# A recurrent scan beside a gated block: opening moments moved to ScalarE, B loaded ahead of the second weight part, fewer warming products

## The chip, the cores and the metric

The kernel runs on one core of one Trainium2 chip. The metric is the device time of one execution in microseconds (us), as the median of several executions. The engines are TensorE (PE; its weight loads are a row of their own, PEld), VectorE (DVE), ScalarE (ACT), GpSimd (POOL) and SyncE (SP), whose queue issues nearly all DMAs here.

## The reference, cut to what matters

The input x has 2048 tokens of 448 features. It is normalised, and the result goes through two branches whose outputs are multiplied and added to x:

```python
def reference(...):
    xn = _layernorm(x, axis=-1)              # (x - mean) / sqrt(var + 1e-5)
    # branch A: complex diagonal recurrence over the tokens, 448 states
    Lam_bar = exp(dt * Lam)
    Bu = xn @ (((Lam_bar - 1) / Lam)[:, None] * Bmat).T
    h[t] = Lam_bar * h[t-1] + Bu[t]
    s = 2 * (h @ Cmat.T).real + xn * Dskip
    # branch B: gated block, 448 -> 1792 -> 448
    z = (sigmoid(xn @ w_gate) * (xn @ w_up)) @ w_down
    return x + s * silu(z)
```

All inputs and the output are bf16.

## The kernel before, in words

The 2048 tokens are cut into four chunks of 512, and each chunk into four tiles of 128 tokens. For a chunk the work is: moments and normalisation of its four tiles, a turn of the normalised tiles into `xnT` (features on the partitions), the gate and up products (14 feature tiles `ft`, a gate bank `g_ps` and an up bank `u_ps` each, `gu_mm` and `emit_gu`), the products with B (`emit_bu`, four state tiles `pt`), the rotations and scans on VectorE, and one chunk later the down products (`emit_down`), the products with C (`emit_y`) and the output.

Every engine runs its instructions in the order in which the Python code emits them; `keep_order` at the end pins that order. Nothing is reordered at run time, so an instruction that waits holds up all that stands behind it on its engine. The same holds for the SP queue, which issues the loads, the transposes by DMA and the stores. Small pieces of work for later chunks are put beside the gate and up products by a planner with fixed costs (`at`, `later`, `fill`); it is not touched here.

The change concerns the opening, that is the first chunk up to its gate and up products.

- **Loads.** SP issues, in this order: x tiles 1 and 2 (one DMA, `x_t[0][:, 0:2]`), x tiles 3 and 4 (one DMA), then `load_w(sync, 0, 512)`: columns 0 to 512 of the gate and up weights (four DMAs, for feature tiles `ft` 0 to 3), `load_w(sync, 512, 1024)` (four DMAs, for `ft` 4 to 7), x of chunk 1 (`load_x(1)`), and B in two halves `b_re` and `b_im` (two DMAs each). ACT issues four small loads of parameter rows. Later SP issues the transposes of B into `bT` (`emit_b`, one for each `pt` and half), with the third weight part, columns 1024 to 1792 (`load_w(sync, 1024, F)`), between those of `pt` 0 and those of `pt` 1.
- **Warming products.** `warm(n)` lets TensorE multiply the identity n times into a bank that nobody reads. There are three groups: 33, 36 and 14 products.
- **Moments.** `ln_stats(t)` takes mean and variance of a tile on VectorE (`bn_stats`, then `bn_aggr`). `ln_root` adds epsilon on VectorE (tile `ve`) and takes the root on GpSimd (`sd`); `ln_scale` takes the reciprocal on VectorE; `ln_norm` normalises on VectorE; `ln_turn` turns a tile on TensorE into the bank `tp_x` (five transposes) and `ln_out` copies it to `xnT`. Tiles 1 and 2 go first, tiles 3 and 4 later.
- **Constants of the scan.** `emit_vecs` turns the parameter rows on TensorE (`tp_v`), copies them on VectorE and takes an exponential on ACT (`dt_b`); `emit_angles` forms `theta`, `turn` and `arg_r` on VectorE. `emit_whole` rounds an angle on ACT, `emit_frac` takes the fraction on VectorE, `emit_sin` and `emit_cos` take sine and cosine on ACT.

TensorE's order in the opening is: 33 warming products, the turn of the rows, 36 warming products, the turns of tiles 1 and 2, 14 warming products, then the products of `ft` 0 and 1 for the first 256 tokens (tiles 1 and 2), the turns of tiles 3 and 4, `ft` 2 and 3 for the first 256 tokens, `ft` 0 to 3 for the other 256, and then whole feature tiles with the products of B between them: `ft` 4, 5, B for `pt` 0, `ft` 6, 7, B for `pt` 1, `ft` 8, 9, B for `pt` 2 and so on.

Of the kernel before, what the change touches and what calls it, by code (L numbers as in the profile page):

```python
# [10 lines left out]
FP32 = mybir.dt.float32  # L11
BF16 = mybir.dt.bfloat16
I32 = mybir.dt.int32
ALU = mybir.AluOpType
ACT = mybir.ActivationFunctionType

S_TOK = 2048
D = 448
F = 1792
P = 128  # L20
TC = 512
HC = TC // 2
NCH = S_TOK // TC
TPC = TC // P
KT = 4
# [5 lines left out]
EPS = 1e-5  # L31
# [32 lines left out]
def kernel(  # L64
# [18 lines left out]
    pe, act, dve, pool, sync = nc.tensor, nc.scalar, nc.vector, nc.gpsimd, nc.sync  # L83
    w = ctx.enter_context(tc.tile_pool(name="w", bufs=1))
# [3 lines left out]
    fp = ctx.enter_context(tc.tile_pool(name="fp", bufs=4))  # L88
# [7 lines left out]
    x_t = [w.tile([P, TPC, D], BF16, name=f"x{c}", tag=f"x{c}") for c in range(3)]  # L96
# [18 lines left out]
    def load_rows(eng, t, mat, f0, f1):  # L115
        eng.dma_start(out=t[:, 0:3, f0:f1], in_=mat[0:384, f0:f1].rearrange("(kt p) f -> p kt f", p=P))
        eng.dma_start(out=t[0:64, 3, f0:f1], in_=mat[384:448, f0:f1])

    def load_w(eng, f0, f1):
        for t, mat, p0 in ((wg, B_w_gate, 0), (wu, B_w_up, 64)):  # L120
            eng.dma_start(out=t[:, :, f0:f1], in_=mat[0:384, f0:f1].rearrange("(kt p) f -> p kt f", p=P))  # L121
            eng.dma_start(out=wt[p0:p0 + 64, f0:f1], in_=mat[384:448, f0:f1])  # L122
# [13 lines left out]
    load_row(act, 3, A_Dskip)  # L136
    sync.dma_start(out=x_t[0][:, 2:4, :], in_=x_src[:, 2:4, :])
    load_w(sync, 0, 512)
    load_w(sync, 512, 1024)
    raw = {}  # L140

    def load_x(c):
        if c == 3:
            x_t.append(w.tile([P, TPC, D], BF16, name="x3", tag="tc_re"))
        sync.dma_start(out=x_t[c][:], in_=x_src[:, c * TPC:(c + 1) * TPC, :])

    load_x(1)
    for nm, mat in (("b_re", A_B_re), ("b_im", A_B_im)):
        raw[nm] = w.tile([P, KT, DP], BF16, name=nm, tag="raw" + nm[1:])
        dve.memset(raw[nm][:, :, D:DP], 0.0)  # L150
        load_rows(sync, raw[nm], mat, 0, D)

    ctr = {}

# [34 lines left out]
    def warm(n):  # L189
        for _ in range(n):  # L190
            pe.matmul(warm_ps[:], lhsT=ident[:], rhs=ident[:], start=True, stop=True)  # L191

    def turn_twice(o, src, n):

        for kt in range(3):
            pe.transpose(o[:, kt, :], src[:, kt * P:(kt + 1) * P], ident[0:n, 0:n])
        pe.transpose(o[:, 3, :], src[:, D - P:D], ident[0:n, 0:n])
        pe.transpose(o[0:64, 3, :], src[:, 384:D], ident[0:n, 0:n])


    mv = w.tile([P, NT, 2], FP32, name="mv")
# [3 lines left out]
    def ln_stats(t):  # L205
        stats = cp.tile([P, 6], FP32, name="stats")
        dve.bn_stats(out=stats[:], in_=x_t[t // TPC][:, t % TPC, :])  # L207
        dve.bn_aggr(out=mv[:, t, :], in_=stats[:])

    def ln_root(c, j0=0, n=TPC, sd=None):  # L210
        t0 = c * TPC + j0
        ve = cp.tile([P, TPC, 1], BF16, name="ve")
        dve.tensor_single_scalar(out=ve[:, 0:n, :], in_=mv[:, t0:t0 + n, 1:2], scalar=EPS, op=ALU.add)
        if sd is None:
            sd = cp.tile([P, TPC, 1], BF16, name="sd")
        pool.tensor_tensor(out=sd[:, j0:j0 + n, :], in0=ve[:, 0:n, :], in1=half[:, 0:n, :], op=ALU.pow)
        return sd
# [33 lines left out]
    def ln_out(j, tp, copy):  # L251
        copy(out=xnT[0][:, :, j * P:(j + 1) * P], in_=tp[:])  # L252


    def emit_b(cc, pt):
        n = P if pt < 3 else 64
        if cc == 0:
            p0 = pt * P
        else:
            p0 = D if pt == 3 else 512 + pt * P  # L260
        sync.dma_start_transpose(out=bT[:, :, p0:p0 + n], in_=raw[("b_re", "b_im")[cc]][0:n, pt, :])
# [13 lines left out]
    def emit_vecs():  # L275
        tp = ps.tile([P, KT, 4], BF16, name="tp_v", tag="g")
        turn_twice(tp, rows, 4)
        vec = w.tile([P, KT, 4], FP32, name="vec")
        dve.tensor_copy(out=vec[:], in_=tp[:])
        dt_b = w.tile([P, KT], BF16, name="dt_b")  # L280
        act.activation(dt_b[:], vec[:, :, 0], ACT.Exp)
        K.update(dt=dt_b, lim=vec[:, :, 1], lre=vec[:, :, 2], dsk=vec[:, :, 3])

    def emit_angles():
        theta, arg_r, turn, r_col = col("theta"), col("arg_r"), col("turn"), col("r_col")
        dve.tensor_tensor(out=theta[:], in0=K["dt"][:], in1=K["lim"], op=ALU.mult)
        dve.tensor_single_scalar(out=turn[:], in_=theta[:], scalar=1.0 / TWO_PI, op=ALU.mult)
        dve.tensor_tensor(out=arg_r[:], in0=K["dt"][:], in1=K["lre"], op=ALU.mult)
        K.update(arg=arg_r)
        K.update(theta=theta, turn=turn, r=r_col)  # L290
# [69 lines left out]
    def emit_whole(pt, eng):  # L360
        whole = sp.tile([P, HC], I32, name="whole", tag=("ta", "tb")[pt % 2])
        if eng is act:
            act.activation(whole[:], iota_f[:], ACT.Copy, scale=K["turn"][:, pt:pt + 1])
        else:
            dve.tensor_scalar(out=whole[:], in0=iota_f[:], scalar1=K["turn"][:, pt:pt + 1], scalar2=None,
                              op0=ALU.mult)
        K[pt] = whole
# [228 lines left out]
    def gu_out(c, ft, gt, ub, ut=None):  # L596
        sig = fp.tile([P, TC], BF16, name="sig")
        act.activation(sig[:], gt[:], ACT.Sigmoid)  # L598
        if ut is up_copy:
            up_copy(ft)  # L600
        elif ut is not None:
            act.copy(out=ub[:], in_=ut[:])  # L602
        emit_mul()

        def mul():
            h = fp.tile([P, TC], BF16, name="hF", bufs=23)
            dve.tensor_tensor(out=h[:], in0=sig[:], in1=ub[:], op=ALU.mult)  # L607
            hF[c, ft] = h

        due.append(mul)  # L610
# [77 lines left out]
    def ln_plan(c):  # L688
        sd, own = [], c - 1
        for j in range(TPC):  # L690
            at(own, 1 + j, 0.8, lambda j=j: ln_stats(c * TPC + j))
            at(own, 7 + j, 0.0, lambda j=j: ln_norm(c, j))
        at(own, 10, 0.0, lambda: ln_twice(c, act.copy))
        at(own, 5, 0.17, lambda: sd.append(ln_root(c)))
        at(own, 6, 0.35, lambda: ln_scale(c, sd[0]))

    dummy = w.tile([P, 1], FP32, name="dummy")
    act.activation(dummy[:], hpi[:], ACT.Exp)
    warm(33)
    ln_stats(0)  # L700
    ln_stats(1)
    emit_vecs()
    warm(36)
    sd0 = ln_root(0, 0, 2)
    ln_stats(2)
    emit_angles()
    tps = {}

    def norm0(j):
        ln_norm(0, j)  # L710
        tps[j] = ln_turn(0, j)
# [1 line left out]
    ln_scale(0, sd0, 0, 2)  # L713
    norm0(0)
    norm0(1)
    warm(14)
    emit_whole(0, act)
    emit_whole(1, act)
    ln_out(0, tps[0], act.copy)
    emit_whole(2, act)  # L720
    emit_whole(3, act)
    act.activation(K["r"][:], K["arg"][:], ACT.Exp)
    ln_stats(3)
    ln_root(0, 2, 2, sd0)
    ln_out(1, tps[1], dve.tensor_copy)
    emit_frac(0)
    emit_sin(0)
# [36 lines left out]
    ln_stats(TPC + 1)  # L764
    gu_out(0, 2, gus[2][0], ubs[2], up_copy)
    gu_out(0, 3, gus[3][0], ubs[3], up_copy)
    for cc in range(2):
        emit_b(cc, 0)
    load_w(sync, 1024, F)
    for pt in range(1, KT):  # L770
        for cc in range(2):
            emit_b(cc, pt)
    sd1 = []

    for j in range(2, TPC):
# [51 lines left out]
    c = NCH - 1  # L827
# [38 lines left out]
```

## Time and profile before

| | |
|---|---|
| median of 3 runs | 199.35 us (198.4 to 199.5) |
| profiled execution, device time | 199.56 us |
| its span, first to last instruction | 197.5 us |
| granted TensorE clock, mean | 1.000 |
| busy: PE, DVE, ACT, POOL | 189.9, 158.3, 109.0, 40.5 us |
| DMA moved | 14.86 MB, mean 75 GB/s |

The profile is one execution. Its times run from the first instruction, and some 2.06 us of the device time (199.56 less 197.5) lie outside the span. A line of the timeline gives the start, the duration, the engine, the line of the kernel and the operation with its tiles; several equal instructions in a row are drawn together with "xN". The chain of waits is followed back from the last instruction: each piece is what the end of the program depended on at that time.

### The profile page before, as it was taken

How to read it: one execution, taken by the hardware profiler on the slowest of the kernel's cores; microseconds unless marked ns; L12 is line 12 of the kernel's file. 1: busy time of each engine (PE TensorE's matmuls, PEld its weight loads, DVE VectorE, ACT ScalarE, POOL GpSimd, SP SyncE). 2: the span in 40 equal slices, each digit the busy share in tenths (PEclk: the TensorE clock that was granted, in tenths of full speed). 3: DMA queues.
4: the chain of work that ended last, by engine and by line, in shares of the span. 5: the costliest groups of instructions: out<-in, count | busy, mean ns of one | idle time of the engine just before them, and what ended most of it. 6: DMA issues, size and time to landing. Idle time of an engine off the chain costs nothing.

```text
span 197.5 us, 3152 instructions
## 1 busy us (share of the span) xinstructions
PE 189.9 (96%) x1093; PEld 92.1 (47%) x1108; DVE 158.3 (80%) x325; ACT 109.0 (55%) x206; POOL 40.5 (21%) x93
## 2 busy tenths in 40 slices
PE   7999979999999999999999999999999999999991
PEld 6965424334444444444444444444444444545561
DVE  4899799784989789999974999999619999994223
ACT  3599646674488886344664766346646644341130
POOL 3337498730302201010232031003200000000000
PEclk9999999999999999999999999999999999999999
DMA  5984984899310310521001001330100010020100
GB/s 156 311 256 98 262 110 95 245 294 184 79 32 0 84 36 27 106 71 27 3 0 28 2 0 27 81 98 23 27 3 0 0 27 2 27 72 24 46 23 23
DMA packets 27591, 14.86 MB, mean 75 GB/s; under 512 B 16308, under 2 KB 27576, under 8 KB 27576
## 3 DMA queue, kind: packets, MB, share of 16 engines
q1 hardware_dynamic: 27568, 14.67, 30.7%
q8 instruction: 8, 0.13, 0.3%
q14 instruction: 7, 0.06, 0.1%
q10 hardware_dynamic: 8, 0.00, 0.0%
HBM read 8.38 MB, written 1.84 MB: 52 GB/s over the span
## 4 chain that ended last, share of the span: by engine, by line
PE 88%; DMA 4%; DVE 3%; SPq 1%; issue 1%; ACT 0%; POOL 0%; ACTq 0%; DVEq 0%; POOLq 0%
PE d_ps L623 21%; PE g_ps L585 17%; PE u_ps L585 16%; PE bu L442 11%; PE y_ps L645 9%; PE g_ps L579 7%; PE warm_ps L191 4%; DMA bT<-b_re 4%; PE y_ps L651 1%; PE y_ps L647 1%; DVE ub L757 1%; SPq L121 1%; SPq L122 0%; DVE xnT L252 0%; PE tp_x L243 0%
## 5 line engine op out<-in xcount | busy, mean ns | idle before, releaser
L598 ACT ACTIVATE sig<-g_ps 128x512 bf16<-128x512 f32 x56 | 33.2, 599 | 35.0 <-PE u_ps L579 35.0
L585 PE MATMUL g_ps<-xnT,wg 128*128 128x512 bf16 (+1 forms) x169 | 45.5, 366 | 0.8 <-issue 0.3
L585 PE MATMUL u_ps<-xnT,wu 128*128 128x512 bf16 (+1 forms) x176 | 45.4, 364 | 0.2
L623 PE MATMUL d_ps<-wd,hF 128*128 128x448 bf16 x224 | 45.0, 352 | 0.0
L602 ACT CAST ub<-u_ps 128x512 bf16<-128x512 f32 x52 | 30.3, 583 | 2.1 <-PE u_ps L585 0.4
L623 PEld LDWEIGHTS <-hF 128*128 128x128 bf16 x224 | 21.6, 98 | 20.4
L442 PE MATMUL bu<-xnT,bT 128*128 128x512 bf16 x112 | 26.8, 379 | 1.2 <-DMA bT<-b_re 1.2
L626 ACT ACTIVATE sigd<-d_ps 128x448 bf16<-128x448 f32 x16 | 8.7, 544 | 33.9 <-PE d_ps L623 33.9
L607 DVE TENSOR_TENSOR hF<-sig,ub 128x512 bf16<-128x512 bf16 x56 | 23.6, 423 | 4.0 <-ACT ub L602 3.6
L585 PEld LDWEIGHTS <-wu 128*128 128x128 bf16 x180 | 17.6, 98 | 18.7
L585 PEld LDWEIGHTS <-wg 128*128 128x128 bf16 x180 | 14.5, 97 | 21.6 <-issue 11.9
L472 DVE TENSOR_TENSOR_SCAN wv<-r_col,st,ta 128x512 bf16<-128x512 f32 x18 | 22.5, 1272 | 0.3
L632 DVE TENSOR_TENSOR g_t<-zb,sigd 128x448 bf16<-128x448 bf16 x16 | 6.2, 390 | 19.1 <-ACT zb L628 19.1
L645 PE MATMUL y_ps<-ct,h 128*128 128x448 bf16 (+1 forms) x102 | 21.0, 341 | 0.0
L442 PEld LDWEIGHTS <-bT 128*128 128x128 bf16 x112 | 10.9, 98 | 14.7 <-DMA bT<-b_re 1.7
L579 PE MATMUL g_ps<-xnT,wt 64*128 64x512 bf16 (+1 forms) x60 | 17.2, 367 | 0.0
L579 PE MATMUL u_ps<-xnT,wt 64*128 64x512 bf16 (+1 forms) x60 | 17.2, 367 | 0.0
L453 ACT CAST bus<-bu 128x512 bf16<-128x512 f32 x24 | 13.7, 586 | 6.0 <-PE bu L442 6.0
L479 POOL TENSOR_TENSOR tq<-wv,smT 128x2 f32<-128x2 bf16 x9 | 3.4, 383 | 62.1 <-DVE wv L472 62.1
L207 DVE BATCH_NORM_STATS2 stats<-x 128x6 f32<-128x448 bf16 x16 | 9.9, 617 | 5.0 <-DMA x<-in_A_x_dram 5.0
L645 PEld LDWEIGHTS <-h 128*128 128x128 bf16 x102 | 9.7, 98 | 8.3
L658 DVE TENSOR_TENSOR sg<-y_ps,g_t 128x448 bf16<-128x448 f32 (+1 forms) x17 | 10.0, 587 | 0.7 <-PE y_ps L651 0.2
(125 smaller groups left out, 212.9 us busy)
## 6 DMA issues: line engine op xcount, KB each, us to landing
out_dram<-o_t SPq DMA_DIRECT2D x15, 112.0 KB, 1.7
wd<-in_B_w_down_dram SPq DMA_DIRECT2D x1, 1568.0 KB, 7.9
x<-in_A_x_dram SPq DMA_DIRECT2D x3, 448.0 KB, 3.5
wg<-in_B_w_gate_dram SPq DMA_DIRECT2D x2, 384.0 KB, 5.2
wu<-in_B_w_up_dram SPq DMA_DIRECT2D x2, 384.0 KB
wg<-in_B_w_gate_dram SPq DMA_DIRECT2D x1, 576.0 KB, 4.5
wu<-in_B_w_up_dram SPq DMA_DIRECT2D x1, 576.0 KB, 6.5
bsw<-bus SPq DMA_DIRECT2D x8, 64.0 KB, 2.1
```

The source lines that it names most:

```text
L207: dve.bn_stats(out=stats[:], in_=x_t[t // TPC][:, t % TPC, :])
L442: pe.matmul(pst[:], lhsT=bT[:, kt, lo:hi], rhs=xnT[c][:, kt, :], start=(kt == 0), stop=(kt == KT - 1))
L453: act.copy(out=bus[:, cc, :], in_=pst[:])
L472: dve.tensor_tensor_scan(out=T["wv"][:, cc, :], data0=rb, data1=T["ta"][:, cc, :], initial=(0.0 if c == 0 else st[pt][:, cc, :]), op0=mul, ...
L579: pe.matmul(t[:, n0:n1], lhsT=wt[p0:p0 + 64, f0:f1], rhs=xnT[c][p0:p0 + 64, KT if c == 0 and p0 else 3, n0:n1], start=first, stop=not first)
L585: pe.matmul(t[:, n0:n1], lhsT=wm[:, kt, f0:f1], rhs=xnT[c][:, kt, n0:n1], start=(not first and kt == 0), stop=(first and kt == 2))
L598: act.activation(sig[:], gt[:], ACT.Sigmoid)
L602: act.copy(out=ub[:], in_=ut[:])
L607: dve.tensor_tensor(out=h[:], in0=sig[:], in1=ub[:], op=ALU.mult)
L623: pe.matmul(d[:], lhsT=hF[c, ft][:, j * P:(j + 1) * P], rhs=wd[:, ft, :], start=(ft == 0), stop=(ft == FT - 1))
L645: pe.matmul(y[:, d0:d1], lhsT=hs[c, pt][:, cc, sl], rhs=ct[:, 2 * pt + cc, d0:d1], start=(pt == 0 and cc == 0), stop=False)
L658: dve.tensor_tensor(out=sg[:, d0:d1], in0=ys[c, j][:, d0:d1], in1=gs[c, j][:, d0:d1], op=ALU.mult)
```

## The change

The moments of tiles 3 and 4 are taken by ACT in three steps instead of by VectorE: a copy with a running sum (`ln_sum`), a scaling of both sums to means (`ln_mean`), and the square of the deviation with a running sum (`ln_square`). The root of tiles 1 and 2 is emitted ahead of the parameter vectors. Both copies of the first two turned tiles are on VectorE (one was on ACT before), behind the epsilon step of tiles 3 and 4, and the four `emit_whole` follow each other on ACT. The warming groups are 26, 22 and 11 products. B is loaded ahead of the second weight part and of x of chunk 1, and the third weight part is issued behind the transposes of B for `pt` 1 instead of `pt` 0.

```diff
     load_w(sync, 0, 512)
-    load_w(sync, 512, 1024)
...
-    load_x(1)
     for nm, mat in (("b_re", A_B_re), ("b_im", A_B_im)):
...
         load_rows(sync, raw[nm], mat, 0, D)
+    load_w(sync, 512, 1024)
+    load_x(1)
...
+    sums = w.tile([P, 2, 2], FP32, name="sums")
+
+    def ln_sum(j):
+        junk = fp.tile([P, TC], BF16, name="junk", tag="sig")
+        act.activation(junk[:, 0:D], x_t[0][:, j, :], ACT.Copy, accum_out=sums[:, j - 2, 0:1])
+
+    def ln_mean():
+        act.activation(mv[:, 2:4, 0:1], sums[:, :, 0:1], ACT.Copy, scale=1.0 / D)
+
+    def ln_square(j):
+        junk = fp.tile([P, TC], BF16, name="junk", tag="sig")
+        act.activation(junk[:, 0:D], x_t[0][:, j, :], ACT.Square, bias=mv[:, j, 0:1], scale=-1.0,
+                       accum_out=sums[:, j - 2, 1:2])
+
-    def ln_root(c, j0=0, n=TPC, sd=None):
+    def ln_root(c, j0=0, n=TPC, sd=None, summed=False):
...
-        dve.tensor_single_scalar(out=ve[:, 0:n, :], in_=mv[:, t0:t0 + n, 1:2], scalar=EPS, op=ALU.add)
+        if summed:
+            dve.tensor_scalar(out=ve[:, 0:n, :], in0=sums[:, :, 1:2], scalar1=1.0 / D, scalar2=EPS,
+                              op0=ALU.mult, op1=ALU.add)
+        else:
+            dve.tensor_single_scalar(out=ve[:, 0:n, :], in_=mv[:, t0:t0 + n, 1:2], scalar=EPS, op=ALU.add)
...
-    warm(33)
+    ln_sum(2)
+    ln_sum(3)
+    warm(26)
     ln_stats(0)
     ln_stats(1)
+    sd0 = ln_root(0, 0, 2)
     emit_vecs()
-    warm(36)
-    sd0 = ln_root(0, 0, 2)
-    ln_stats(2)
+    ln_mean()
+    warm(22)
+    ln_square(2)
+    ln_square(3)
     emit_angles()
...
     norm0(0)
     norm0(1)
-    warm(14)
-    emit_whole(0, act)
-    emit_whole(1, act)
-    ln_out(0, tps[0], act.copy)
-    emit_whole(2, act)
-    emit_whole(3, act)
+    warm(11)
+    for pt in range(KT):
+        emit_whole(pt, act)
     act.activation(K["r"][:], K["arg"][:], ACT.Exp)
-    ln_stats(3)
-    ln_root(0, 2, 2, sd0)
+    ln_root(0, 2, 2, sd0, True)
+    ln_out(0, tps[0], dve.tensor_copy)
     ln_out(1, tps[1], dve.tensor_copy)
...
-    for cc in range(2):
-        emit_b(cc, 0)
-    load_w(sync, 1024, F)
-    for pt in range(1, KT):
+    for pt in range(KT):
         for cc in range(2):
             emit_b(cc, pt)
+        if pt == 1:
+            load_w(sync, 1024, F)
```

## The prediction, made before the changed kernel ran

> **What bounds the kernel now.** I read the page's busy times first, then the chain of waits, then the timeline of the opening and the windows.
>
> ```profile
> PE 189.9 (96%) x1093; PEld 92.1 (47%) x1108; DVE 158.3 (80%) x325; ACT 109.0 (55%) x206; POOL 40.5 (21%) x93
> ```
>
> TensorE is idle for 7.6 of 197.5 us. In the chain, and in PE's waits from 26 to 190 us, one hole stands out; the rest is the start, the end and short issue gaps:
>
> ```profile
> PE bu L442 <- DMA bT<-b_re: 1.2, 1, 1.2
> ```
> ```profile
> 8.20 0.56 PE tp_x L243 x10
> 8.76 0.78 PE warm_ps L191 x14
> 9.54 0.38 PE g_ps L585 x3
> ...
> 17.17 0.58 SPq L121
> 17.81 0.48 SPq L122
> 18.33 0.59 SPq L121
> 18.96 0.49 SPq L122
> 19.50 6.99 DMA bT<-b_re
> 26.54 1.90 PE bu L442 x8
> ```
>
> So time can come from two places. Real products begin at 9.44 us (timeline), and all before that on PE is warming or turning. And B for `pt` 1 waits until 26.5 us for a transpose that SP issued at 19.50, behind the third weight part (17.17 to 19.45), and that took 6.99 us to land. Between the two PE has no other wait, so both should add up.
>
> The timeline shows what the start hangs on:
>
> ```profile
> 5.51 0.16 DVE L213 TENSOR_SCALAR ve<-mv 128x2 bf16<-128x2 f32 x1
> 5.58 0.62 DVE L207 BATCH_NORM_STATS2 stats<-x 128x6 f32<-128x448 bf16 x1
> 5.63 0.21 ACT L281 ACTIVATE dt_b<-vec 128x4 bf16<-128x4 f32 x1 [2.03 <-DVE vec L279]
> 5.76 0.73 POOL L216 TENSOR_TENSOR sd<-ve,half 128x2 bf16<-128x2 bf16 x1 [3.44 <-DVE ve L213]
> 6.85 0.70 DVE L230 TENSOR_SCALAR xn<-x,mv,rsd 128x448 bf16<-128x448 bf16 x2
> 8.04 0.72 PE L243 MATMUL tp_x<-ident,xn 128*128 128x128 bf16 x10
> 8.80 0.49 DVE L252 COPY xnT<-tp_x 128x640 bf16<-128x640 bf16 x1 [0.29 <-PE tp_x L243]
> ```
>
> The tiles are normalised by 7.55, but PE turns them at 8.04, because its second warming group ends then. The second copy ends at 9.29 and PE starts 0.15 later.
>
> **The change, part by part.**
>
> *Warming.* The 33 weight loads of the first group take 3.44 us, 0.104 each; the 14 of the third take 0.82, 0.059 each. The 36 of the second take 2.72, which is 13 at the slow pace and 23 at the fast one: the pace rises near 6.7 us. The granted clock is 1.00 in all rows, so only durations show this (mean 313 ns for the first 33, 219 ns for the last 14). With 26 the first group ends at 1.35 + 2.71 = 4.06, and the turn of the rows follows 0.19 later as before, at 4.25. When the rows land isn't shown: not after 4.98, when they are read. Their last issue ends at 2.07 and the shortest landings in the page are 1.5 to 1.7 us, so not before 3.6. I take no wait, since that bound is the nearer small transfer; at 4.98 the turn would come where it is now. The second group runs from 4.59, 22 at 0.105, to 6.90; the turns start at 6.95.
>
> *Root first.* The second `bn_aggr` ends at 5.02. `ve` stood 0.49 behind it, now it follows at 5.06; GpSimd starts 0.25 later, at 5.31, and ends at 6.04. VectorE meanwhile copies `vec` (to 5.31), waits for `dt_b` and makes three angle steps, to about 6.05. Reciprocal 6.08 to 6.24, normalisation from 6.27: xn 1 at 6.62, xn 2 at 6.97. So PE, at 6.95, finds the first tile ready and the second as it gets there.
>
> *Moments on ACT.* VectorE loses two `bn_stats` and two `bn_aggr`, 2 x (0.62 + 0.18) = 1.6 us, and gains one copy of 0.45. ACT gains four passes over 448 elements and one tiny step (0.20, as `dt_b`), and loses the copy of 0.69. The passes aren't in the trace. Nearest rows: 0.53 (`zb`, 448 elements, no pointer), 0.68 (`c_tmp`, one pointer), 0.77 (`xn` on ACT, two pointers); a running sum that is read out separately may add a tiny step of 0.20, so 0.53 to 0.97. No gain below 0.53 is possible, since all three rows have at least this many elements or more operands. I take 0.68, one pointer being what the square has. x of tiles 3 and 4 is issued at 1.23 and lands 2.7 us later, at 3.95; ACT is idle from 3.60 to 5.63. Sums 4.0 to 5.36, `dt_b` to 5.57, means to 5.77, squares to 7.13. Here the change adds a wait: the `ve` of tiles 3 and 4 stands on VectorE ahead of both copies to `xnT`, and PE waits for these. By 0.68 `ve` ends at 7.34, and the first copy can't start before 6.95 + 0.48 = 7.43 anyway (0.48 from first turn to first copy, as now), so the wait is hidden. From 0.71 a pass on it isn't, and each further 0.1 costs 0.4.
>
> [...]
>
> *Copies and start.* Two copies on VectorE take 0.89 (timeline, those of tiles 3 and 4): 7.43 to 8.32. PE starts 0.15 later, at 8.47, against 9.44: **0.97 us gained**. The 11 products end at 8.1. The weights of `ft` 0 to 3 keep their places in the queue: gate is there by 6.95 (SP waited for it) and up by 8.65 (SP issued on its semaphore without a wait), 0.15 before the first up product. Bounds of this term: 0.5 if the rows land as late as 4.98; 0.3 if the turns and the third group run slow (21 at 0.104 from 6.95 end at 9.13); nothing with 0.97 a pass, when squares end at 8.3 and PE starts at 9.55. Behind it ACT keeps step: angles 7.1 to 8.9, table load from 9.1 (10.12 now), the first sigmoid at 15.4 (16.32 now), for a bank PE wants at 16.0 (16.97 now).
>
> *Loads.* SP waits for one landing in eight DMAs back, so its pace (last load issued 9.82 to 10.3) hardly moves; only the order does.
>
> ```profile
> 10.30:14.50 4.20, 4.20 (x46) 2.97 (x42) 3.87 (x14) 4.12 (x9) 0.99 (x4) 1.00 0.85 266
> 14.50:17.20 2.70, 2.70 (x27) 1.91 (x25) 2.64 (x8) 2.67 (x6) 2.70 (x8) 1.00 0.28 59
> 17.20:19.50 2.30, 2.25 (x12) 0.79 (x12) 2.27 (x6) 1.91 (x5) 1.32 (x4) 1.00 0.61 107
> ```
>
> The last two columns are DMA share and GB/s. The loads are through by 14.5; then the DMA engines stand at 0.28 and 0.61 while SP issues two transposes (1.3 us each) and the third weight part. With B first, its 2.1 MB (448 KB x, 896 KB weights, 784 KB B) are in by about 10, as 1.8 MB are by 8.2 at 262 GB/s. SP can issue the four transposes of `pt` 0 and 1 from 10.4 to 15.6, five us of idle SP. B for `pt` 1, wanted at 25.3 - 0.97 = 24.3, is then long there: **1.21 us gained**.
>
> What comes late next? The second weight part is issued 7.5 to 9.7 instead of 4.0 to 7.4. In those places B took 6.2 to 6.3 us, so it lands by 13.8 to 16.0; `ft` 4 wants gate at 16.0, up at 16.7, the rest at 17.3. x of chunk 1, issued at 9.82, lands by 16.1 (same 6.3); VectorE wants it at 15.1 to 15.3, behind two `ub` copies: a stall of up to 0.9 there. Behind it stand the copy of `u_ps` for `ft` 2 and 3, which free banks for B; they would end by 18.9, and PE wants that bank at 20.1. The third weight part is issued at 15.6 to 18 (17.17 to 19.45 now) and took 4.5 to 6.5 us, so it lands by 24.5; `ft` 8 wants it at 26.1. Transposes of `pt` 2 and 3 follow from 18, B wants them at 29.3.
>
> *Later.* PE runs 2.2 us earlier. VectorE idles 1.0 at 35 us and 3.2 at 44 (waiting for x of chunk 2, which SP reaches 3 us earlier), then 0.84 and 1.43 before the scan of chunk 0 is needed at 72.7. That covers it.
>
> **The sum.** 0.97 + 1.21 = 2.18; 199.56 - 2.18 = 197.4 us, in terms of the profiled execution, which is 0.2 above the median of 199.35. Own range of this case: 196.6 (the lowest of the three runs lies 0.95 under their median; I allow 0.8) to 198.1 (the start gains 0.3).
>
> **Rivals.**
>
> *ACT's passes are dear.* At 0.97 a pass the start gains nothing and only the 1.21 stay: 198.3. For it: the accumulator has no row here. Against: three rows up to 0.77, at which PE still starts at 8.75.
>
> *The wait changes its place.* Third part or second part comes late and `ft` 8 or 4 waits for what B no longer waits for: 0.97 stay, 198.6. For it: a load behind transposes took 6.5 us here and a transpose behind loads 7.0. Against: 1.6 us of reserve and the idle DMA share above. Both rivals at once: about 199.5, no change.
>
> *PE stays slow (slower than before).* The pace rose after 5.3 us of unbroken warming. 24 products fewer, a gap while the rows are turned, and another where PE outruns VectorE might leave it slow in the real products. A 256-column product takes 0.109 us at the fast pace (3 in 0.33); at the slow one it would be twice that by the ratio 0.104 to 0.059, roughly. So each us of slow real work loses 0.5, and the 2.2 gained are lost if the slow pace lasts 4.4 us beyond 8.5, to about 12.9. To 15 it would cost 3.3 less 2.2: 200.7. Against: the gaps that I count are 0.2 to 0.7 us, and PE is busy for all but these from 1.35 on.
>
> [...]
>
> **How the numbers follow.** Forecast 0.62, dear passes 0.12, displaced wait 0.08, neither gain 0.05, slow PE 0.13. Half a per cent (1.0 us) is about what a measurement can tell: faster means under 198.35, slower over 200.35. The forecast, two fifths of the dear passes and a quarter of the displaced wait make faster 0.69; slow PE makes slower 0.13; same is 0.18. The range goes from the forecast's low end, 196.6, to 199.5, where both gains fail; it leaves out the slow case and a little below.
>
> **What would show it.** Right: the first `g_ps` product near 8.5; four ACT passes of 0.55 to 0.7; `ve` of tiles 3 and 4 done before the first turn is; no wait of B on `bT`; PE's first down product near 43.5 (45.7 now). Wrong: a PE wait for weights at 16 or 26 us, VectorE's first copy held by the squares, or products of `ft` 0 at twice 0.109 us.

## The result and the profile after

The changed kernel takes 197.33 us (median of 7 runs, 196.91 to 197.60), the kernel before 198.63 us beside it (7 runs, 198.16 to 199.50). The ratio is 0.9927, with a 95% interval of 0.9904 to 0.9951: faster by 0.5 to 1.0%, about 1.45 us. The profiled execution took 197.33 us with a span of 195.5 us, 2.0 us under the span of before. In the experiments further down, four executions (one of `b0_base`, one of `p2_opening`, two of `f3_opening`) lay over 1.5% above the fastest of their kernel; medians, ranges and ratios leave them out.

The page's busy times after, to be held against those of before:

```profile
PE 188.8 (97%) x1069; PEld 90.7 (46%) x1084; DVE 156.8 (80%) x322; ACT 111.0 (57%) x214; POOL 42.3 (22%) x93
```

PE's busy time falls by 1.1 us, for the most part warming (before the first real product PE is busy for 6.75 us, 8.09 before); the rest of the span's 2.0 is idle time that has gone. The timeline of the opening after (start, duration, engine, line, operation):

```profile
4.04 0.58 ACT L214 ACTIVATE junk<-x 128x448 bf16<-128x448 bf16 x1 [0.44 <-DMA x<-in_A_x_dram]
4.52 0.19 ACT L214 ACTIVATION_READ_ACCUMULATOR junk<-x 128x1 f32 x1
...
5.04 0.17 DVE L231 TENSOR_SCALAR ve<-mv 128x2 bf16<-128x2 f32 x1
...
5.30 0.73 POOL L234 TENSOR_TENSOR sd<-ve,half 128x2 bf16<-128x2 bf16 x1 [2.98 <-DVE vec L297]
...
5.65 0.67 ACT L221 ACTIVATE junk<-x,mv 128x448 bf16<-128x448 bf16 x1
...
6.27 0.70 DVE L248 TENSOR_SCALAR xn<-x,mv,rsd 128x448 bf16<-128x448 bf16 x2
...
6.72 0.76 PE L261 MATMUL tp_x<-ident,xn 128*128 128x128 bf16 x10
6.88 0.19 ACT L221 ACTIVATION_READ_ACCUMULATOR junk<-x,mv 128x1 f32 x1
...
7.10 0.17 DVE L228 TENSOR_SCALAR ve<-sums 128x2 bf16<-128x2 f32 x1
7.21 0.89 DVE L270 COPY xnT<-tp_x 128x640 bf16<-128x640 bf16 x2
...
8.15 0.49 PE L603 MATMUL g_ps<-xnT,wg 128*128 128x256 bf16 x3
```

The root of tiles 1 and 2 runs at 5.30 (5.76 before), the normalisation at 6.27 (6.85), the turns at 6.72 (8.04), the copies at 7.21, and real products begin at 8.15 (9.44). The squares end at 7.07 with the read of the accumulator, 0.03 ahead of the epsilon step that stands on VectorE before the copies.

The chain of waits after (start, duration, what), to be held against the one of before:

```profile
6.24 0.83 ACT junk L221 x3
7.27 0.84 DVE xnT L270 x2
8.15 0.49 PE g_ps L603 x3
...
24.11 1.73 PE bu L460 x8
...
43.08 2.65 PE d_ps L641 x14
...
86.99 2.65 PE d_ps L641 x14
...
126.19 0.62 PE g_ps L603 x3
126.81 2.44 DMA xnT<-xn
129.25 0.05 issue
129.30 0.82 PE g_ps L603 x3
...
134.43 2.65 PE d_ps L641 x14
```

The same products in the chain of before:

```profile
45.69 2.65 PE d_ps L623 x14
...
89.31 2.65 PE d_ps L623 x14
...
136.40 2.65 PE d_ps L623 x14
```

The 6.99 us for B's transposes are off the chain, and B for `pt` 1 follows without a hole. There are new pieces: ACT's squares lie on the chain at 6.24, and a turned tile of chunk 3 at 126.81. So the lead over before isn't constant. By the starts of the down products in the two chains it is 2.61 us at chunk 0 (45.69 before, 43.08 after), 2.32 at chunk 1 (89.31, 86.99), and 1.97 at chunk 2 (136.40, 134.43). Some 0.64 us are given back, at the first products of chunks 2 and 3. For chunk 3 the chain names a tile turned by DMA; for chunk 2 it names nothing, and that a turned tile is late there too is an inference.

DMA share and GB/s (last two columns of the windows) after:

```profile
14.50:17.20 2.70, 2.65 (x21) 1.31 (x21) 1.78 (x5) 2.63 (x5) 2.70 (x8) 1.00 0.96 144
17.20:19.50 2.30, 2.30 (x14) 0.93 (x14) 2.27 (x6) 1.81 (x4) 0.07 (x1) 1.00 0.59 129
```

From 14.5 to 17.2 us the engines' share was 0.28 before and is 0.96 now: the transposes for `pt` 1, which SP issues at 14.21 and 15.52, fall into the stretch, and the end of the loads with them (x of chunk 1 is there at 15.8).

### The profile page after: what moved, and what is told of

Read it like the earlier page. It is cut to its first block, busy times and chain, and to the rows that moved or that the text cites. A ratio compares the mean times of both kernels' runs of the same rounds, so it can differ in the third digit from the quotient of the medians.

```text
span 195.5 us, 3111 instructions
## 1 busy us (share of the span) xinstructions
PE 188.8 (97%) x1069; PEld 90.7 (46%) x1084; DVE 156.8 (80%) x322; ACT 111.0 (57%) x214; POOL 42.3 (22%) x93
## 4 chain that ended last, share of the span: by engine, by line
PE 91%; DMA 3%; DVE 2%; issue 1%; ACT 1%; POOL 0%; ACTq 0%; DVEq 0%
PE d_ps L641 22%; PE g_ps L603 20%; PE u_ps L603 18%; PE bu L460 12%; PE y_ps L663 8%; PE g_ps L597 8%; PE y_ps L669 1%; DMA x<-in_A_x_dram 1%; PE y_ps L665 1%; DMA xnT<-xn 1%; DVE stats L207 1%; DVE xnT L270 0%; ACT junk L221 0%; DVE sg L676 0%; POOL sd L234 0%
## 5 line engine op out<-in xcount | busy, mean ns | idle before, releaser
L603 PEld LDWEIGHTS <-wg 128*128 128x128 bf16 x180 | 14.5, 98 | 22.3 <-issue 12.3
L597 PE MATMUL g_ps<-xnT,wt 64*128 64x512 bf16 (+1 forms) x60 | 17.2, 367 | 0.0
L597 PE MATMUL u_ps<-xnT,wt 64*128 64x512 bf16 (+1 forms) x60 | 17.2, 367 | 0.0
L497 POOL TENSOR_TENSOR tq<-wv,smT 128x2 f32<-128x2 bf16 x9 | 4.1, 450 | 57.6 <-DVE wv L490 57.6
L207 DVE BATCH_NORM_STATS2 stats<-x 128x6 f32<-128x448 bf16 x14 | 8.6, 617 | 5.8 <-DMA x<-in_A_x_dram 5.8
```

What stands on the lines that cost most here:

```text
L597: pe.matmul(t[:, n0:n1], lhsT=wt[p0:p0 + 64, f0:f1], rhs=xnT[c][p0:p0 + 64, KT if c == 0 and p0 else 3, n0:n1], start=first, stop=not first)
L603: pe.matmul(t[:, n0:n1], lhsT=wm[:, kt, f0:f1], rhs=xnT[c][:, kt, n0:n1], start=(not first and kt == 0), stop=(first and kt == 2))
```

## The experiments

In all of them the turns by DMA are replaced by plain copies of the same tiles, so that values of the output differ. No part of the change was timed by itself with the turns by DMA in place, so what a part is worth is shown for these stand-ins. In the first base a turn is two copies of 64 partitions; in the second base this holds for B alone, while C and the normalised tiles have one copy each. In both, the opening behaves as in the kernels above: two copies take SP 1.25 to 1.34 us, a turn 1.20 to 1.30, and B for `pt` 1 waits 1.38 and 1.44 us in the bases (1.21 before). Ratios are to the kernel before, run beside each group on the same chip, and kernels of different groups are compared by ratio; "start" is the first real product and "B 1" the first product of B for `pt` 1 in the profiled execution.

| kernel | median us (range) | ratio (95%) | start | B 1 (wait) |
|---|---|---|---|---|
| b0_base, first base | 199.74 (198.3 to 200.9) | 1.0043 (1.0015 to 1.0071) | 8.89 | 26.14 (1.38) |
| a0_changed | 198.24 (197.8 to 199.1) | 0.9974 (0.9958 to 0.9991) | 8.51 | 24.22 (0) |
| p1_loads | 198.06 (197.7 to 198.9) | 0.9967 (0.9951 to 0.9983) | 9.04 | 24.75 (0) |
| p2_opening | 200.17 (199.0 to 202.0) | 1.0077 (1.0047 to 1.0107) | 8.17 | 25.67 (1.63) |
| f0_base, second base | 198.85 (198.1 to 199.9) | 1.0023 (0.9998 to 1.0047) | 9.04 | 26.36 (1.44) |
| f1_changed | 196.83 (196.6 to 197.1) | 0.9910 (0.9882 to 0.9939) | 8.57 | 24.28 (0) |
| f2_loads | 198.10 (197.4 to 198.9) | 0.9969 (0.9949 to 0.9990) | 9.40 | 25.13 (0) |
| f3_opening | 198.74 (197.8 to 200.6) | 1.0021 (0.9989 to 1.0053) | 8.09 | 25.47 (1.51) |
| g1_warm83 | 197.47 (196.7 to 198.7) | 0.9946 (0.9926 to 0.9966) | 8.35 | 24.06 (0) |
| g2_no_warm | 199.14 (197.8 to 199.8) | 1.0025 (1.0003 to 1.0046) | 8.56 | 26.92 (0) |
| g3_two_more_passes | 197.61 (197.6 to 197.7) | 0.9946 (0.9931 to 0.9961) | 9.15 | 24.86 (0) |
| g4_moments_dve | 197.47 (197.4 to 197.8) | 0.9940 (0.9926 to 0.9955) | 9.02 | 24.73 (0) |

**First base: both kernels, and each half of the change.** The edit common to all, for B:

```diff
-        sync.dma_start_transpose(out=bT[:, :, p0:p0 + n], in_=raw[...][0:n, pt, :])
+        for h in range(2):   # 64 partitions each
+            sync.dma_start(out=bT[64 * h:64 * h + 64, :, p0:p0 + n], in_=src[q:q + 64, pt, :]...[:, :, c0:c0 + n])
```

> The base of the experiments: the kernel before, with each turn by DMA (B, C and the normalised tiles of chunks 1 to 3) replaced by two plain copies of the same tile, of 64 partitions each, in the same place in the queue. The values of the output differ by that. Both theories: a copy of 64 x 512 takes SP about 0.5 to 0.6 us to issue (as the swaps of halves), so two take 1.0 to 1.2, against 1.3 for a turn, and the third weight part is issued within 0.5 us of 17.2. If the landing behind that part is what holds B for pt 1, PE still waits there, 0.3 to 1.5 us; products begin at 9.4. Time within 1 us of the kernel before. If the turn itself is what is slow, the wait is gone.

> The changed kernel with the same replacement of turns by plain copies (values differ by that). Theory: products begin at 8.15, B for pt 1 does not wait, and the gain over the base is 1.3 us (the start) plus what the base waits for B, 1.6 to 2.5 in all, less what the starts of chunks 2 and 3 wait for their tiles. Rival (the gain of the change hangs on how turns by DMA crowd the queue): less than 0.8 us.

The loads alone take the base and move B and the second weight part; the opening alone takes the changed kernel and puts the loads back:

```diff
 # p1_loads, on the base
     load_w(sync, 0, 512)
-    load_w(sync, 512, 1024)
-    load_x(1)
     ...                      # B
+    load_w(sync, 512, 1024)
+    load_x(1)
 # and the third part behind the copies of pt 1; p2_opening: the reverse on the changed kernel
```

> The base (turns as plain copies) with the new order of loads alone; moments, root and 83 warming products as before. Theory (two causes): products begin at 9.4, the wait for B goes, and the gain is what the base waits there. Rival (late weights take the gain): a wait at ft 4 or ft 8, gain under 0.3 us.

> The changed kernel (turns as plain copies) with the old order of loads: only moments on ACT, early root, copies and 59 warming products are new. Theory (B lands at a time that the loads alone set, so the two gains do not add): products begin at 8.15, but B for pt 1 comes at the same time as in the base, the wait there grows by about 1.3, and the time stays within 0.4 us of the base. Rival (the gains add, as my prediction had it): the wait is as in the base and 1.0 to 1.3 us are gained.

The base shows the wait of before, in PE's waits of `b0_base`:

```profile
PE bu L451 <- DMA bT<-b_re: 1.4, 1, 1.4
```

The loads alone take it away and gain 1.7 us in the medians (1.5 by the ratios), close to the 1.38 that the base waits. The opening alone starts 0.7 us earlier and gains nothing (200.17 against 199.74). My expectation for it was off: the wait for B grew by 0.25 us and not by 1.3, for B came 0.47 earlier than in the base. The rest of its lead went at the starts of chunks 2 and 3, where PE stands 0.59 and 0.65 us (0.2 in all in `b0_base`). Adding the opening to the loads gains nothing either here (198.24 against 198.06), and the whole change gains 1.5, a little under the 1.6 to 2.5 expected. PE's waits of `a0_changed` say where its lead went:

```profile
PE g_ps L612 <- issue: 1.0, 3, 0.7
PE g_ps L612 <- DMA out_dram<-o_t: 0.9, 1, 0.9
```

PE stands 0.65 and 0.91 us at the starts of chunks 2 and 3, where `p1_loads` has 0.2 in all. The eight copies of chunk 3 take SP 6.04 us. That this is the base's own doing, by its doubled copies, is an inference; the second base tests it (2.71 us for four copies in `f1_changed`).

**Second base.** The same four kernels with one copy for a tile of C or of x:

```diff
-        sync.dma_start_transpose(out=xnT[c][:, 0:KT, cols], in_=xb[:, j, :])
+        sync.dma_start(out=xnT[c][:, 0:KT, cols], in_=xb[:, j, :].rearrange("p (a b) -> p a b", a=KT))
```

> A second base, closer to the kernel before in its later part: the turns of B as two plain copies each (as in the first base), but those of C and of the normalised tiles as one plain copy each, so that SP's semaphores rotate there as in the kernel before; a constant fills the 32 top partitions of C's tiles first (the output's values differ by the copies). Theory: opening as in the kernel before, B for pt 1 waits 1.2 to 1.6 us on its landing; no waits at the starts of chunks 2 and 3, since one copy takes SP half as long as a turn. Time within 0.5 us of the kernel before. Rival (the copies shift the loads): the wait for B is under 0.5.

> The changed kernel on the second base. Theory (0.7 to 1.3 at the start by the moment at which TensorE's pace rises, 1.2 to 1.6 from B, and what the chunk starts took back, 0.6, was due to the turns' time on SP): 1.9 to 2.6 us under its base, no wait at a chunk start. Rival (the opening's gain is lost later whatever the turns take): 1.2 to 1.6, as the loads alone would give.

> The second base with the new order of loads alone (old opening, 83 warming products). Theory: what the base waits for B is gained, 1.2 to 1.6 us. Rival (weights late at ft 4 or 8): under 0.5.

> The second base with the new opening alone (old order of loads). Theory (B's landing is set by the loads): the wait for B grows to 1.6 to 2.6 and no more than 0.5 us is gained. Rival (the gains add): 0.8 to 1.3 us gained and the wait as in the base.

The whole change gains 2.02 us, the loads alone 0.75, the opening alone nothing (198.74 against 198.85, with executions up to 200.6 that the base hasn't). So in times the opening is worth 1.27 with the new loads (1.17 by the ratios) and nothing without. The loads alone missed the 1.2 to 1.6 that I expected: 0.75 in the medians, 1.07 by the ratios, though in the profiles B for `pt` 1 comes 1.23 earlier. PE's waits of `f3_opening` and of `f1_changed`:

```profile
PE bu L467 <- DMA bT<-b_re: 1.5, 1, 1.5
```
```profile
PE tp_x L263 <- DVE xn L250: 0.8, 1, 0.8
PE g_ps L610 <- issue: 0.3, 2, 0.2
PE g_ps L610 <- DVE xnT L272: 0.2, 1, 0.2
```

With the old loads the wait for B is there at any start. My expectation for `f3_opening` was off in its profile, though: the wait was 1.51 and not 1.6 to 2.6, since B landed 0.9 us earlier than in the base (25.47 against 26.36). SP shows a cause: in the base it issued the third weight part at 17.91, here at 16.73; in the base it had stood 1.3 us for `b_im` to land, and here it didn't. So this profile kept its early start, and its execution took 198.21 us against 199.24 for the base's. That landing differs between executions (25.5 to 26.5 in five profiles); why the median gains nothing isn't settled. And `f1_changed` has no wait at a chunk start, and its gain is the largest: what the changed kernel gives back there goes with the time of the turns on SP, 1.5 us each at chunks 2 and 3 (5.84 and 6.04 us for four, 5.13 and 5.35 before). Why these took longer after the change isn't settled.

**The warming products.**

```diff
-    warm(26) ... warm(22) ... warm(11)
+    warm(33) ... warm(36) ... warm(14)     # g1_warm83;  g2_no_warm: none of the three
```

> The changed kernel on the second base, with the old warming groups (33, 36, 14) in place of 26, 22, 11. Theory (in the new opening PE must be free when the tiles are normalised at 6.3 to 7.0): the second group ends at 7.2 to 8.0 by the moment at which the pace rises, products begin at 8.7 to 9.4 instead of 8.1 to 8.6, and 0.5 to 0.9 us are lost against the changed kernel. Rival (the start hangs on VectorE and the landing of x alone): under 0.2 us lost.

> The changed kernel on the second base without any warming product: the rival of a slow TensorE taken to its end. Slow-PE theory: the turns and the products after 8 us run at about twice their durations (a product of 256 columns spaced by 0.21 us instead of 0.109) until some 5 us of work have passed, to about 12 to 13 us, and 2.0 to 2.8 us are lost. Its rival (the products wait for VectorE and loads anyway): under 1 us lost.

With 83 products the ratio is 0.0036 higher, 0.7 us, near the two intervals' width and within the 0.5 to 0.9 expected. Its profile doesn't show that loss: the execution took 196.78, and in it the pace had risen early: 36 products in 2.18 us, where before took 2.89, and a start at 8.35. Its slowest took 198.7: a range of 2.0 us over 12 executions, against 0.5 over 6 with 59 products and the same loads (`f1_changed`); in the first base, 59 products with the new loads ranged over 1.3 us (`a0_changed`). With none, TensorE's row in the timeline of `g2_no_warm` is:

```profile
6.73 1.25 PE L263 MATMUL tp_x<-ident,xn 128*128 128x128 bf16 x10 [2.18 <-DVE xn L250]
8.56 0.80 PE L610 MATMUL g_ps<-xnT,wg 128*128 128x256 bf16 x3 [0.58 <-DVE xnT L272]
9.15 0.85 PE L610 MATMUL u_ps<-xnT,wu 128*128 128x256 bf16 x3
...
12.79 0.85 PE L610 MATMUL g_ps<-xnT,wg 128*128 128x256 bf16 x3
13.43 0.85 PE L610 MATMUL u_ps<-xnT,wu 128*128 128x256 bf16 x3
14.21 0.33 PE L604 MATMUL g_ps<-xnT,wt 64*128 64x256 bf16 x1
```

Three products are 0.6 us apart instead of 0.33 until 14.2, with the granted clock at 1.00 in that window too. B for `pt` 0 comes at 21.96 instead of 19.32, and the ratio is 0.0115 higher, 2.3 us: the whole gain. Slow pace is the rival that can undo the change, and it takes 5.7 us of slow real work. The loss is as that theory had it; the pace rose later than the 12 to 13 us it gave.

**ACT's passes and where the moments are.**

```diff
 # g3_two_more_passes, in ln_square
+        act.activation(junk[:, 0:D], x_t[0][:, j, :], ACT.Copy)
         act.activation(junk[:, 0:D], x_t[0][:, j, :], ACT.Square, bias=..., accum_out=...)
 # g4_moments_dve
-    ln_sum(2); ln_sum(3); ln_mean(); ln_square(2); ln_square(3)
+    ln_stats(2)                   # in the place of the squares
-    ln_root(0, 2, 2, sd0, True)
+    ln_stats(3)
+    ln_root(0, 2, 2, sd0)
```

> The changed kernel on the second base with one more ACT pass over 448 elements ahead of each of the two squares (its result is overwritten). Theory (the first copies to xnT stand on VectorE behind the step that waits for the squares, and the start has no slack there): two passes of 0.56 less their overlap, about 1.0 us, go straight to the start, products begin at 9.1 to 9.6, 0.9 to 1.1 us lost. Rival (the wait is hidden behind the turns, as my prediction had it up to 0.3 us): 0.7 or less.

> The changed kernel on the second base with the moments of tiles 3 and 4 back on VectorE (statistics of tile 3 ahead of the angles, of tile 4 ahead of the epsilon step), all else as changed: early root, 59 warming products, copies on VectorE, new loads. Theory (the 1.6 us of VectorE are what the start gains): products begin near 9.4 to 9.6 and 0.9 to 1.3 us are lost, about the time of the new loads alone. Rival (early root and fewer warming products bring the start): under 0.5 us lost.

VectorE in the timeline of `g3_two_more_passes`, and then of `g4_moments_dve`:

```profile
8.14 0.17 DVE L231 TENSOR_SCALAR ve<-sums 128x2 bf16<-128x2 f32 x1 [1.20 <-ACT junk L224]
8.21 0.88 DVE L273 COPY xnT<-tp_x 128x640 bf16<-128x640 bf16 x2
```
```profile
7.14 0.62 DVE L209 BATCH_NORM_STATS2 stats<-x 128x6 f32<-128x448 bf16 x1
7.79 0.18 DVE L210 BATCH_NORM_AGGREGATE mv<-stats 128x2 f32<-128x6 f32 x1
8.01 0.17 DVE L233 TENSOR_SCALAR ve<-mv 128x2 bf16<-128x2 f32 x1
8.09 0.88 DVE L272 COPY xnT<-tp_x 128x640 bf16<-128x640 bf16 x2
```

The two added passes move the copies by exactly 1.0 us against the changed kernel (7.21) and the start to 9.15: no slack was left. In times 0.7 are lost, which is the most that the rival allowed and less than the theory's 0.9 to 1.1, for in `f1_changed` the start isn't always at 8.15 either. In its profile the second half of x landed 0.6 later (ACT's first sum at 4.62 instead of 4.04), which pushed `dt_b`, the angles and the normalisation behind it, to a start at 8.57. With the moments on VectorE the start is 9.02 and 0.6 us are lost (expected: 0.9 to 1.3, or under 0.5 by the rival). By both readings this edit carries about half or more of the opening's gain, though the intervals of the two ratios overlap. The early root and the copies were not tried alone.

None of these runs points to a version that beats the changed kernel; turning the tiles of chunks 2 and 3 earlier would be the next thing to try, and has no measurement.

## Why the prediction was right, point by point

**The mechanism** held: the start moved by 1.29 us and the wait for B went, both by the steps named. Four of the signs given appeared: first products near 8.5 (8.15), passes of 0.55 to 0.7, no wait on `bT`, the first down product at 43.1 for 43.5. The fifth did not quite: `ve` of tiles 3 and 4 ends at 7.27 (7.10 and 0.17), and the first tile's turn is done by 7.20 (6.72 and the 0.48 from first turn to first copy). And one of the signs of being wrong, the first copy held by the squares, is there: the chain goes from the squares to the copies, at no cost in this profile and with 0.34 us of idle VectorE in `f1_changed`.

**That the time agrees to 0.07 us** (197.33 against 197.4) is in part luck. The sum started from 199.56, which is 0.93 above the median of seven (198.63); from that median it would have given 196.45. The gain by the ratio is 1.45 us, two thirds of the 2.18 forecast. Between the two profiled executions it is 2.23: the start gave 0.32 more than forecast, the chunk starts took 0.64 that the sum had at nothing, and 0.23 of the difference lies outside the spans (2.06 before, 1.83 after).

**The start**, 0.97 forecast, 1.29 seen. 22 products took 2.14 us, not 2.31, as the pace rose within them, so the turns came at 6.72 for 6.95; the copies followed 0.49 later as forecast, and the first product comes 0.05 after them, not 0.15. Those 0.15 were no delay behind the copy: in the chain of before, the start hangs on the 14 products of the third warming group. The rows were there when PE asked for them. A pass with its read costs 0.57 or 0.67 from start to start (0.58 and 0.67 plus 0.19, with overlap): 0.68 was right for the squares, high for the sums; without the read a sum took 0.56 and 0.58, a square 0.65 and 0.67.

**The base of the sum** was the weak term. I took 2.18 us off the profiled 199.56, slower than any of the seven runs of before (198.16 to 199.50), and named only 0.2 as its distance to the median. In old openings the products began at 8.89, 9.04, 9.04, 9.40 and 9.44 (five profiles of five kernels), in the new one at 8.09, 8.15, 8.17, 8.51 and 8.57: by the middle values 0.87 apart. The pace of PE rose between about 2.7 us after the first product (`g1_warm83`: rows turned at 4.61 instead of 4.98, which is 8 fast products) and about 6 us, as the timeline of `a0_changed` shows:

```profile
4.56 2.53 PE L193 MATMUL warm_ps<-ident 128*128 128x128 bf16 x22
6.88 0.93 PE L265 MATMUL tp_x<-ident,xn 128*128 128x128 bf16 x10
7.57 0.89 DVE L274 COPY xnT<-tp_x 128x640 bf16<-128x640 bf16 x2 [0.31 <-PE tp_x L265]
```

There all 22 products and some of the turns are slow, and the copies wait 0.31 for the turns. A second group of 36 products makes the start follow the moment at which the pace rises; with 22 it clearly does so in one of seven profiles, this one. So of the 0.97 some 0.3 was that one execution of before (9.44 against 9.16, the mean of the five), and over seven runs each the range narrows from 1.3 us to 0.7.

What sets the moment at which the pace rises is shown by none of the runs.

**"Both should add up"** holds for the pair alone. The opening without the new loads gains nothing in the medians of either base. That the wait for B takes the lead is not shown: in the profiles PE began 0.72 and 0.95 us earlier and B for `pt` 1 came 0.47 and 0.89 earlier, so the wait took 0.25 and 0.07. In the first base the starts of chunks 2 and 3 took more; in the second the cause is open.

**"Later ... that covers it"** failed: I looked at VectorE's idle time and not at the turns by DMA, and chunks 2 and 3 begin 0.64 us late in all, a term that the sum had at nothing. In the result it was hidden by the larger gain at the start and the slow execution that the sum began from.

**The smaller bounds** held but for one. SP's last load was issued at 9.90 (9.82 before), in both behind one wait of 1.2 us for the first gate weights to land. VectorE waited 0.89 for x of chunk 1 (up to 0.9 forecast). The up weights, which I gave a margin of 0.15, were waited for by 0.18 (PEld at 8.54), since the start came 0.32 earlier than forecast. The slow rival's price, 0.5 for each us of slow work, was measured: B for `pt` 0 came 2.64 us later than in `f1_changed`, from the same start, after 5.7 us of slow work.

## What to carry to other kernels

Two stalls in a row on one engine needn't add: here the early start was worth over 1 us with the later stall removed and nothing with it in place, in the medians of the second base. So measure each half of such a change alone before adding them, and look in more than one profile for where the lead goes. Make the sum of a change against several executions or bound how far one profile may lie off, and read from the durations which part of it varies. When an engine runs ahead by two microseconds, check all who feed it later, the DMA queue too.

## What the runs showed of the hardware

A pass on ACT with a running sum is two instructions in these traces: in the profile after, the pass takes 0.56 to 0.67 us for 448 elements and the read of the accumulator 0.19 us (0.18 in `g1_warm83`). There the read overlaps its own pass and the next one by about 0.1 us each, so that passes follow each other at 0.57 and 0.67 us. TensorE's pace rose (in the profile before from 0.104 to 0.059 us for a weight load) at a moment that varied from about 2.7 us (`g1_warm83`) to about 6 us (`a0_changed`) after the first of a row of warming products. The granted clock reads 1.00 in the windows around it in the profiles before and after, and 1.00 as the mean of the other two executions; only durations show it.
